# Expert routing beside matmuls: four-byte operands of full height for the search's products, and another order around the first routing

## The chip, the cores and the metric

The kernel runs on one core of a Trainium2 chip. The metric is the device time of one execution in microseconds (us). The engines have short names in the profile: PE is TensorE (matmuls; PEld is its weight loading), DVE is VectorE, ACT is ScalarE, POOL is GpSimd, and SP is SyncE, which issues most DMA transfers.

## What is computed

Three blocks follow each other over 3072 tokens of width 512. The first is a linear attention with decay. The second, which the change is about, gives each token to one of 8 experts, with at most 384 tokens for each expert, and runs that expert's two matmuls on them. The third is a rational activation between two more matmuls.

```python
def _moe_ref(x, w_gate, w1, w2):
    N, D = x.shape                       # 3072, 512
    E = w_gate.shape[1]; cap = N // E    # 8, 384
    flat = (x @ w_gate).flatten()
    order = np.argsort(-flat)
    assigned = -np.ones(N); counts = np.zeros(E)
    for idx in order:                    # best pairs of token and expert first
        tok, e = idx // E, idx % E
        if assigned[tok] >= 0 or counts[e] >= cap:
            continue
        assigned[tok] = e
        counts[e] += 1
    ...
    for e in range(E):
        h = np.maximum(x[assigned == e] @ w1[e], 0.0)
        out[assigned == e] = h @ w2[e]

# behind it, for all tokens: h = x @ w_in; P = a0 + a1 h + a2 h^2 + a3 h^3
# Q = 1 + |b0| |h| + |b1| h^2; result = (P / Q) @ w_out
```

## The kernel before

**The three stretches.** Up to about 180 us the attention runs, 24 blocks of 128 tokens. From about 180 to 202 us the first expert's tokens are found, with little else to do. From there on the eight experts follow each other, n = 0 to 7: each time 384 tokens are gathered from DRAM (`fetch`, one indirect DMA on POOL per 128 tokens), transposed on PE (`xt`), multiplied by `w1` (`mm1`, 8 pieces f of 12 matmuls) and `w2` (`mm2`, 8 pieces of 12), then by `w_in` (`mm3`, 16 pieces of 12), and, after the activation on ACT, DVE and POOL, by `w_out` (`mm4`, 16 pieces of 9). Each float32 operand is split in two parts of the type `float32r` (in the code `F32R`, four bytes a number, a rounded float32), so every product is made of three.

**The search.** An expert is full when 384 tokens have it as their best. `route(n)` finds the n-th expert that fills, and the score at which it does, bit by bit, because the greedy order is one threshold per expert. For n from 1 on, it takes 8 rounds of 4 bits, so 56 rounds in all; the searches follow each other without a pause, ahead of the experts that need them, and the last ends within expert 6. In a round DVE compares the scores of all tokens with 16 thresholds (`cm`, 128 x 24 x 16). PE counts per expert: three products with the one-hot `oh` as the weights, 64 columns wide (8 blocks times 8 experts, L609). DVE takes the diagonal (`cmk`), adds (`ce`) and spreads it (`ex`, 64 rows). PE sums over the 64 rows with a product whose weights are ones (`oneb[0:64]`, 128 columns, L623). DVE takes the largest, and sets the next threshold (`thr`, `pre`). After the 8 rounds come a pair of products for ranks (L660, L661), three for positions (L691) and one to spread the list (L707); the result is `idx`, the list of tokens, and `ei`, the expert's number.

**What sets the order.** PE, ACT and POOL execute in the order in which the code is written; DVE's order is chosen by a scheduler, and `tc.issue_after(x)` puts what it holds behind x. The search is a generator, `Chain`; a `hop` issues two of its steps, so that a round is two hops. `slot()` makes a hop after a piece of an expert's matmuls whenever a credit reaches 1. Before the slots begin, `HOPS0` says how many hops stand before the transposes of the first expert, after them, and after its first `mm1`.

**Other work beside the first expert.** Weights of `w_out` come as float64: `job_conv` turns a block into float32 (L240, L242, L243 on DVE, L241 on ACT), and `job_split` splits it (L246 on ACT, L247 on POOL). `w1_split` and `w2_split` do the same split for the expert's weights.

## Time and profile before

| | |
|---|---|
| median of 3 runs | 1106.55 us (1105.77 to 1111.75) |
| the profiled execution | 1109.52 us, of which the span of its instructions is 1107.6 us |
| PE | 1034.6 us busy (93%), 6278 matmuls |
| DVE, ACT, POOL | 792.7 us (72%), 697.4 us (63%), 635.3 us (57%) |
| the chain that ended last | PE 72%, of it the search's L609 and L623 1% each by the page |
| granted PE clock, mean | 0.971 |

The chain that ended last is followed back from the last instruction to what released each step; the shares are of the span. The granted clock is given as a share of 2.4 GHz: 1.00 is 2.4 and 0.50 is 1.2 GHz.

### The profile page before, as it was taken

Reading aid. Unit: us, or ns where it says so; the run is one execution under the profiler, and the core shown is the slowest. Engines: PE = TensorE matmul, PEld = TensorE weight load, DVE = VectorE, ACT = ScalarE, POOL = GpSimd, SP = SyncE. Lnnn points to the kernel's source line nnn. Section 1 sums busy time; section 2 is a strip of 40 time slices with the busy share of each in tenths; the row PEclk is TensorE's granted clock in tenths of the full one; section 3 lists DMA queues with packets and bytes.
Section 4 is the critical chain, followed back from the end, with each engine's and each line's share of the span. In section 5 each row is a group of like instructions: output and inputs, shape, how many; then the busy total and the mean of one; then the engine's idle time right before and its main releaser. Section 6 shows DMA issues by size and latency. Waiting matters only on the chain.

```text
span 1107.6 us, 18242 instructions
## 1 busy us (share of the span) xinstructions
PE 1034.6 (93%) x6278; PEld 918.2 (83%) x6278; DVE 792.7 (72%) x1850; ACT 697.4 (63%) x1365; POOL 635.3 (57%) x612
## 2 busy tenths in 40 slices
PE   6988985589999999999999999999999999999995
PEld 6877874478778988898889888988898889989994
DVE  5899897677985688568847874787578855761673
ACT  7988782245685387448844874478348735873783
POOL 5766762373586356635763566356636664666452
PEclk9999997599899999999999999999999999999998
DMA  9998862332334312331233123212321232224110
GB/s 195 239 259 219 215 163 87 115 124 77 97 109 129 105 39 86 103 98 39 86 105 95 39 86 112 89 44 81 115 86 58 67 115 86 59 67 124 57 58 28
DMA packets 142027, 115.00 MB, mean 104 GB/s; under 512 B 56560, under 2 KB 122352, under 8 KB 141936
## 3 DMA queue, kind: packets, MB, share of 16 engines
q1 hardware_dynamic: 131184, 76.10, 26.4%
q0 software_dynamic: 10752, 37.75, 10.5%
q8 instruction: 49, 0.80, 0.3%
q14 instruction: 42, 0.34, 0.1%
HBM read 98.10 MB, written 15.73 MB: 103 GB/s over the span
## 4 chain that ended last, share of the span: by engine, by line
PE 72%; DVE 5%; issue 1%; POOL 1%; DMA 1%; ACT 1%; POOLq 0%; DVEq 0%
PE w L795 35%; PE acc L888 22%; PE acc L795 12%; PE pr L609 1%; PE w L779 1%; PE pr L623 1%; DMA xg<-xd,idx 1%; DVE t L868 0%; DVE acc L867 0%; DVE t L851 0%; DVE t L850 0%; DVE qq L866 0%; POOL woh L247 0%; POOL qq L849 0%; DVE cm L573 0%
## 5 line engine op out<-in xcount | busy, mean ns | idle before, releaser
L888 PE MATMUL acc<-woh,hg 128*128 128x512 f32 x1152 | 292.7, 400 | 5.0 <-ACT hg L873 4.2
L888 PEld LDWEIGHTS acc<-woh,hg 128*128 128x128 f32 x1152 | 214.0, 189 | 49.6 <-ACT hg L873 5.4
L849 POOL TENSOR_TENSOR qq<-qq,z 128x384 f32<-128x384 f32 x127 | 128.9, 1015 | 164.7 <-ACT z L847 164.7
L874 POOL TENSOR_TENSOR hg<-t,hg 128x384 fp32r<-128x384 f32 x127 | 131.1, 1032 | 91.8 <-ACT hg L873 62.1
L795 PE MATMUL w<-yT,wih 128*128 128x384 f32 x960 | 178.6, 338 | 0.0
L795 PEld LDWEIGHTS w<-yT,wih 128*128 128x128 f32 x960 | 166.8, 188 | 4.6 <-DVE yT L820 0.2
L795 PE MATMUL w<-xT,w1s 128*128 128x384 f32 x768 | 152.4, 347 | 0.5 <-ACT xT L781 0.5
L795 PE MATMUL acc<-hg,w2s 128*128 128x384 f32 x768 | 148.5, 342 | 0.1
L795 PEld LDWEIGHTS w<-xT,w1s 128*128 128x128 f32 x768 | 135.8, 192 | 4.4 <-ACT xT L781 0.7
L795 PEld LDWEIGHTS acc<-hg,w2s 128*128 128x128 f32 x768 | 133.4, 189 | 3.4 <-DVE hg L804 0.5
L247 POOL TENSOR_TENSOR w1s<-w1r,w1s 128x512 fp32r<-128x512 f32 x64 | 83.3, 1301 | 71.9 <-ACT w1s L246 71.4
L247 POOL TENSOR_TENSOR w2s<-w2r,w2s 128x512 fp32r<-128x512 f32 x64 | 84.2, 1316 | 54.6 <-ACT w2s L246 54.4
L873 ACT ACTIVATE hg<-t 128x384 fp32r<-128x384 f32 x128 | 67.2, 525 | 75.6 <-DVE t L868 75.5
L866 DVE SCALAR_TENSOR_TENSOR qq<-qq,acc 128x384 f32<-128x384 f32 x128 | 70.8, 553 | 59.6 <-ACT acc L861 34.9
L795 PE MATMUL w<-yT,wis 128*128 128x384 f32 x576 | 111.1, 341 | 0.0
L795 PEld LDWEIGHTS w<-yT,wis 128*128 128x128 f32 x576 | 100.9, 189 | 2.8
L846 ACT ACTIVATE qq<-w,rb 128x384 f32<-128x384 f32 x128 | 73.1, 571 | 32.3 <-PE w L795 31.4
L803 ACT ACTIVATE hg<-w 128x384 fp32r<-128x384 f32 x64 | 31.3, 489 | 94.2 <-PE w L795 83.2
L850 DVE TENSOR_TENSOR t<-w,t 128x384 f32<-128x384 f32 x128 | 70.4, 550 | 23.8 <-ACT t L848 23.8
L246 ACT ACTIVATE w2s<-w2r 128x512 fp32r<-128x512 f32 x64 | 40.2, 629 | 73.9 <-POOL w1s L247 33.1
L848 ACT ACTIVATE t<-w,ab 128x384 f32<-128x384 f32 x128 | 86.1, 672 | 0.0
L860 ACT ACTIVATE z<-qq,qcb 128x384 f32<-128x384 f32 x128 | 77.5, 606 | 6.8 <-POOL qq L849 6.8
(174 smaller groups left out, 1731.1 us busy)
## 6 DMA issues: line engine op xcount, KB each, us to landing
wis<-wid POOLq DMA_DIRECT2D x42, 512.0 KB, 3.6
w1r<-in_moe_w_dram SPq DMA_DIRECT2D x64, 256.0 KB, 2.9
w2r<-in_moe_w_dram SPq DMA_DIRECT2D x64, 256.0 KB, 2.7
qn<-in_q_dram SPq DMA_DIRECT2D x48, 128.0 KB, 4.1
kn<-in_k_dram SPq DMA_DIRECT2D x24, 256.0 KB, 4.4
vn<-in_v_dram SPq DMA_DIRECT2D x24, 256.0 KB, 4.9
xd<-xn SPq DMA_DIRECT2D x48, 128.0 KB, 3.9
raw<-in_moe_w_in_dram SPq DMA_DIRECT2D x10, 512.0 KB, 5.6
```

Source lines behind the costliest of these rows:

```text
L246: nc.scalar.activation(dst[:, 0], src, AF.Copy)
L247: lo_eng.tensor_tensor(dst[:, 1], src, dst[:, 0].bitcast(F32), op=OP.subtract)
L795: nc.tensor.matmul(o, w[a], x[b], start=first and n[key] == 1, stop=last and n[key] == total)
L846: nc.scalar.activation(qq, p, AF.Square, scale=rb)
L848: nc.scalar.activation(t, p, AF.Identity, bias=ab[:, 2:3], scale=ab[:, 3:4])
L849: light(n, i).tensor_tensor(qq, qq, z, op=OP.add)
L850: nc.vector.tensor_tensor(t, p, t, op=OP.mult)
L860: nc.scalar.activation(z, qq, AF.Ln, bias=qcb)
L866: nc.vector.scalar_tensor_tensor(qq, qq, QC, r, op0=OP.add, op1=OP.mult)
L873: nc.scalar.activation(g[:, 0], t, AF.Copy)
L874: light(n, i).tensor_tensor(g[:, 1], t, g[:, 0].bitcast(F32), op=OP.subtract)
L888: nc.tensor.matmul(ACC[t], g[:, x, t * 128:(t + 1) * 128], woh[:, i, y], start=i == 0 and x + y == 0, stop=i == NF2 - 1 and x == 1)
```

## The change

For n from 1 on, the operands of the search's counting and summing products and of the rank products become `F32R`: new tiles `ohr` (one-hot), `oner` (ones), `umor` (a matrix for ranks), and `cm`, `ex` and `X` in the new type. `ex` gets 128 rows, of which the lower 64 are set to zero once, and the ones of the sum (`oner`) all 128 rows. The counting product keeps its 64 columns of weights. `pre` and, in the last round, the comparison with the capacity live in PSUM. For the first routing (n = 0) the two-byte types stay, and its thresholds move from PSUM to SBUF.

The order around the first routing is another: the updates of `Tm` and `Sl`, which prepare the next search, and the first step of the next search stand behind `idx`; the gathers stand ahead of the first splits; `HOPS0` goes from (3, 1, 1) to (1, 2, 1), one hop fewer in all; and each `job_conv(f)` stands behind the low part of the activation of piece f + 1 (`HLO`).

```diff
-HOPS0 = (3, 1, 1)
+HOPS0 = (1, 2, 1)
...
+    ppre = prb[:, 264:296].bitcast(I32)
...
+    oner = rt.tile([128, 128], F32R, name="oner")
+    umor = rt.tile([128, 128], F32R, name="umor")
+    ohr = rt.tile([128, NCH, E], F32R, name="ohr")
+    ex = rt.tile([128, E, 2 ** BITS_REST[0]], F32R, name="ex")
+    nc.vector.tensor_copy(ex[64:128].rearrange("p e j -> p (e j)"), zero[64:128, 0:1].to_broadcast([64, E * 2 ** BITS_REST[0]]))
+    nc.vector.tensor_copy(oner, oneb)
+    nc.vector.tensor_copy(umor, half("umo", BF16))
...
-            nc.vector.tensor_tensor(oh, t8, mraw[:, :, None].to_broadcast([128, NCH, E]), op=OP.is_equal)
+            nc.vector.tensor_tensor(ohr, t8, mraw[:, :, None].to_broadcast([128, NCH, E]), op=OP.is_equal)
...
-                    pre = rt.tile([128, J], I32, name="pre")
+                    pre = ppre[:, 0:J] if n else rt.tile([128, J], I32, name="pre")
...
-                thr = pthr[:, 32 * (i % 2):32 * (i % 2) + J]
+                thr = pthr[:, 32 * (i % 2):32 * (i % 2) + J] if n else rt.tile([128, J], I32, name="thr", bufs=2)
...
-                cm = rt.tile([128, NCH, J], BF16, name="cm")
+                cm = rt.tile([128, NCH, J], F32R if n else BF16, name="cm")
...
                 for g in range(3):
                     nc.tensor.matmul(pc.rearrange("p c j -> p (c j)"),
-                                     oh[:, 8 * g:8 * g + 8, :].rearrange("p c e -> p (c e)"),
+                                     ohr[:, 8 * g:8 * g + 8, :].rearrange("p c e -> p (c e)"),
                                      cm[:, 8 * g:8 * g + 8, :].rearrange("p c j -> p (c j)"),
...
-                ex = rt.tile([64, E, J], FP16, name="ex")
...
-                nc.vector.tensor_tensor(ex, ce[:, None, :].to_broadcast([64, E, J]),
+                nc.vector.tensor_tensor(ex[0:64], ce[:, None, :].to_broadcast([64, E, J]),
...
                 pd = pr(128, E, J)
-                nc.tensor.matmul(pd.rearrange("p e j -> p (e j)"), oneb[0:64, :], ex.rearrange("p e j -> p (e j)"),
+                nc.tensor.matmul(pd.rearrange("p e j -> p (e j)"), oner, ex.rearrange("p e j -> p (e j)"),
                                  start=True, stop=True)
...
-                    fe = rt.tile([128, E, J], F32, name="fe")
-                    nc.vector.tensor_scalar(fe, pd, float(CAP), None, op0=OP.is_ge)
+                    nc.vector.tensor_scalar(pd, pd, float(CAP), None, op0=OP.is_ge)
                     S = rt.tile([128, E], F32, name="S")
-                    nc.vector.tensor_reduce(S, fe, axis=AX.X, op=OP.add)
+                    nc.vector.tensor_reduce(S, pd, axis=AX.X, op=OP.add)
...
-        X = rt.tile([128, 2, NCH], BF16, name="X")
+        X = rt.tile([128, 2, NCH], F32R, name="X")
...
-        nc.tensor.matmul(pw[:, 0], half("umo", BF16), Xf, start=True, stop=True)
-        nc.tensor.matmul(pw[:, 1], oneb, Xf, start=True, stop=True)
+        nc.tensor.matmul(pw[:, 0], umor, Xf, start=True, stop=True)
+        nc.tensor.matmul(pw[:, 1], oner, Xf, start=True, stop=True)
...
-        eo = rt.tile([128, E], F32, name="eo")
-        nc.vector.tensor_scalar(eo, c8, em, None, op0=OP.is_equal)
-        nc.vector.tensor_scalar(sl[:, 0], u, float(CAP), BIG, op0=OP.is_lt, op1=OP.mult)
-        nc.vector.tensor_tensor(Tm, sl[:, 0], Tm, op=OP.add)
-        nc.vector.scalar_tensor_tensor(Sl, eo[:, None, :].to_broadcast([128, NCH, E]), BIG, Sl,
-                                       op0=OP.mult, op1=OP.add)
...
-        nc.vector.tensor_scalar(idx, ix, float(NT // 2), None, op0=OP.add)
+        LASTI[0] = nc.vector.tensor_scalar(idx, ix, float(NT // 2), None, op0=OP.add).ins
+
+        with tc.issue_after(LASTI[0]):
+            eo = rt.tile([128, E], F32, name="eo")
+            nc.vector.tensor_scalar(eo, c8, em, None, op0=OP.is_equal)
+            nc.vector.tensor_scalar(sl[:, 0], u, float(CAP), BIG, op0=OP.is_lt, op1=OP.mult)
+            nc.vector.tensor_tensor(Tm, sl[:, 0], Tm, op=OP.add)
+            nc.vector.scalar_tensor_tensor(Sl, eo[:, None, :].to_broadcast([128, NCH, E]), BIG, Sl,
+                                           op0=OP.mult, op1=OP.add)
...
-        nc.vector.scalar_tensor_tensor(h[:, 1], p, 0.0, h[:, 0].bitcast(F32), op0=OP.max, op1=OP.subtract)
+        HLO[n, f] = nc.vector.scalar_tensor_tensor(h[:, 1], p, 0.0, h[:, 0].bitcast(F32), op0=OP.max,
+                                                   op1=OP.subtract).ins
...
         pass
     begin(0)
+    for t in range(TB):
+        fetch(0, t)
     w1_split(0, 0)
     w1_split(0, 1)
-    for t in range(TB):
-        fetch(0, t)
     for f in range(2):
         w2_split(0, f)
-    chain = Chain()
+    with tc.issue_after(LASTI[0]):
+        chain = Chain()
...
             if n == 0:
                 job_split(f - 1)
-                job_conv(f)
+                with tc.issue_after(HLO[0, min(f + 1, NF1 - 1)]):
+                    job_conv(f)
```

On PE, around the first expert's transposes (`w<-cft,xg`): this is what stood there from the transposes on to the second `mm1` piece (`w<-xT,w1s`); L609 is the counting product, L623 the summing one.

```order
L779 MATMUL w<-cft,xg 128x128 x12
L623 LDWEIGHTS oneb
L623 MATMUL pr<-ex,oneb 128x128
L795 MATMUL w<-xT,w1s 128x384 x12
L609 LDWEIGHTS oh
L609 MATMUL pr<-cm,oh 64x128
L609 LDWEIGHTS oh
L609 MATMUL pr<-cm,oh 64x128
L609 LDWEIGHTS oh
L609 MATMUL pr<-cm,oh 64x128
L795 MATMUL w<-xT,w1s 128x384 x12
```

The same place on PE after the change, where L621 is the counting product, L634 the summing one, L791 the transposes and L807 the experts' products:

```order
L621 MATMUL pr<-cm,ohr 64x128 x3
L791 MATMUL w<-cft,xg 128x128 x12
L634 MATMUL pr<-ex,oner 128x128
L621 MATMUL pr<-cm,ohr 64x128 x3
L807 MATMUL w<-xT,w1s 128x384 x12
L634 MATMUL pr<-ex,oner 128x128
L807 MATMUL w<-xT,w1s 128x384 x12
```

A sum and a count now stand between the transposes and the first `mm1` piece, where only a sum stood; the separate weight loads are gone from the list, since a product of this type issues its own.

On POOL, between the last conversions of the attention stretch (`wih`) and the second expert weights (`w2s`), the gathers (`xg<-xd,idx`) move:

```order
 L247 TENSOR_TENSOR wih<-cv_2361,wih 128x512
 L247 TENSOR_TENSOR wih<-cv_2416,wih 128x512
+L756 DMA xg<-xd,idx 128x512 x3
 L247 TENSOR_TENSOR w1s<-w1r,w1s 128x512 x2
-L744 DMA xg<-xd,idx 128x512 x3
 L247 TENSOR_TENSOR w2s<-w2r,w2s 128x512 x2
```

They stood behind the two splits of `w1s`, and stand ahead of them.

On DVE, in the middle of the first expert (before): L804 is the low part of an `mm1` piece, L240, L242 and L243 are a `w_out` conversion, and the rest are the search's steps.

```order
L618 TENSOR_REDUCE ce<-cmk 64x16
L242 SCALAR_TENSOR_TENSOR xg<-yT,xg 128x512
L619 TENSOR_TENSOR ex<-ce,pr 64x128
L243 ISA xg<-xg 128x1024
L633 TENSOR_REDUCE fs<-pr 128x16
L240 TENSOR_SCALAR xg<-yT 128x512
L634 TENSOR_SCALAR fs,nf<-fs 128x15
L804 SCALAR_TENSOR_TENSOR hg<-w,hg 128x384
L567 SCALAR_TENSOR_TENSOR pr<-nf,pre 128x16
L242 SCALAR_TENSOR_TENSOR xg<-yT,xg 128x512
L573 TENSOR_TENSOR cm<-m,pr 128x384
```

The same conversion (the fifth) on DVE after the change, where L818 is the low part of the activation:

```order
L818 SCALAR_TENSOR_TENSOR hg<-w,hg 128x384
L628 TENSOR_TENSOR cmk<-pr,cft 64x128
L240 TENSOR_SCALAR xg<-yT 128x512
L629 TENSOR_REDUCE ce<-cmk 64x16
L242 SCALAR_TENSOR_TENSOR xg<-yT,xg 128x512
L630 TENSOR_TENSOR ex<-ce,pr 64x128
L643 TENSOR_REDUCE fs<-pr 128x16
L644 TENSOR_SCALAR fs,nf<-fs 128x15
L579 SCALAR_TENSOR_TENSOR pr<-nf,pr 128x16
L585 TENSOR_TENSOR cm<-m,pr 128x384
```

The conversion stood inside the threshold part of a round, and stands inside its counting part.

## Rows read from the trace of the kernel before

**Rows 1.** Windows: length, then PE, PEld, DVE, ACT, POOL busy (count), clock, DMA.

```profile
817.80:926.30 108.50, 108.50 (x577) 96.45 (x577) 74.31 (x188) 67.87 (x131) 62.36 (x63) 1.00 0.27 81
926.30:1027.80 101.50, 101.50 (x542) 94.91 (x541) 54.02 (x96) 67.74 (x131) 62.40 (x63) 1.00 0.26 79
```

**Rows 2.** Timeline of PE in expert 3: start us, duration us, what, count.

```profile
575.71 0.35 PE L609 MATMUL pr<-cm,oh 128*64 128x128 bf16 x3
...
580.75 0.35 PE L609 MATMUL pr<-cm,oh 128*64 128x128 bf16 x3
...
588.37 0.23 PE L623 MATMUL pr<-ex,oneb 64*128 64x128 f16 x1
...
590.74 2.25 PE L795 MATMUL acc<-hg,w2s 128*128 128x384 f32 x12
592.82 0.20 PE L660 MATMUL pr<-X,cit 128*128 128x48 bf16 x1
...
595.08 2.25 PE L795 MATMUL acc<-hg,w2s 128*128 128x384 f32 x12
```

**Rows 3.** Timeline of PE in expert 5, with four transposes.

```profile
877.18 2.26 PE L888 MATMUL acc<-woh,hg 128*128 128x512 f32 x9
879.28 0.60 PE L779 MATMUL w<-cft,xg 128*128 128x128 f32 x4
...
881.81 2.25 PE L888 MATMUL acc<-woh,hg 128*128 128x512 f32 x9
883.99 0.23 PE L623 MATMUL pr<-ex,oneb 64*128 64x128 f16 x1
```

**Rows 4.** Timeline of PE in the attention, two blocks, one without the L393 products.

```profile
63.03 1.68 PE L380 MATMUL pa<-QB,kh 128*128 128x256 f32 x12
64.64 0.69 PE L393 MATMUL ps<-vt,kn 128*64 128x64 f32 x16
65.26 1.19 PE L422 MATMUL pt<-IW,xt 128*128 128x136 f32 x8
66.29 1.05 PE L405 MATMUL py<-qt,Sb 128*128 128x128 f32 x8
...
85.14 1.66 PE L380 MATMUL pa<-QB,kh 128*128 128x256 f32 x12
86.64 1.09 PE L422 MATMUL pt<-IW,xt 128*128 128x136 f32 x8
87.57 1.05 PE L405 MATMUL py<-qt,Sb 128*128 128x128 f32 x8
```

**Rows 5.** Groups by form, whole span: count | busy us, mean ns | idle before.

```profile
L380 PE MATMUL pa<-QB,kh 128*128 128x256 f32 x288 | 43.6, 301 | 1.2 <-POOL QB L365 0.8 <-DVE kh L369 0.2
...
L422 PE MATMUL pt<-IW,xt 128*128 128x136 f32 x192 | 28.8, 294 | 0.7 <-ACT xt L412 0.7
```

**Rows 6.** Timeline, the first expert's start; in brackets idle time and its releaser.

```profile
201.64 0.19 DVE L714 TENSOR_SCALAR idx<-ix 128x3 int32<-128x3 f32 x1
...
203.31 0.29 DVE L633 TENSOR_REDUCE fs<-pr 128x16 f32<-128x128 f32 x1 [0.35 <-PE pr L623]
...
204.38 1.15 POOL L744 DMA_INDIRECT xg<-xd,idx  x1 [0.17 <-DVE pre L564]
204.49 0.55 DVE L573 TENSOR_TENSOR cm<-m,pr 128x384 bf16<-128x384 f32 x1
...
207.09 0.95 POOL L744 DMA_INDIRECT xg<-xd,idx  x1 [0.30 <-issue]
...
212.62 4.21 PE L795 MATMUL w<-xT,w1s 128*128 128x384 f32 x12 [0.47 <-ACT xT L781]
```

**Rows 7.** Windows beside the first expert: columns as in the first group.

```profile
241.20:245.30 4.10, 0.15 (x1) 0.11 (x1) 3.78 (x8) 1.71 (x3) 4.10 (x4) 0.93 0.11 42
245.30:252.74 7.44, 7.44 (x28) 7.02 (x27) 3.12 (x7) 0.49 (x1) 0.52 (x1) 0.58 0.00 0
```

**Rows 8.** Timeline of DVE in the first of these windows.

```profile
241.47 1.48 DVE L240 TENSOR_SCALAR xg<-yT 128x512 int32<-128x512 int32 x1 [0.99 <-POOL woh L247]
```

More of the change, by code (lines that the diff above doesn't have):

```diff
@@ L535, in pr @@
         return v
+    oner = rt.tile([128, 128], F32R, name="oner")
[5 more added lines that the diff above has]
+    nc.vector.tensor_copy(umor, half("umo", BF16))
     ROUTE = {}
+    LASTI = {}
     def route(n):
@@ L577, in route @@
                 o2, b2, _ = CI_OFF[tb, i + 1]
-                pre = rt.tile([128, 2 ** b2], I32, name="pre")
+                pre = ppre[:, 0:2 ** b2] if n else rt.tile([128, 2 ** b2], I32, name="pre")
                 nc.vector.tensor_tensor(pre, cit[:, o2:o2 + 2 ** b2], thr[:, 0:1].to_broadcast([128, 2 ** b2]),
@@ L693, in route @@
         yield
-        Zm = rt.tile([128, NB, 8], F32, name="Zm")
+        Zm = rt.tile([128, NB, 8], F32, name="cmk")
         Z = rt.tile([128, NB], FP16, name="Z")
@@ L795, in three @@
             nc.tensor.matmul(o, w[a], x[b], start=first and n[key] == 1, stop=last and n[key] == total)
+    HLO = {}
     def mm1(n, f):
```

## The prediction

> **What bounds the kernel now.** The first view to read is the windows that hold one expert's worth of work each, from one `yT` to the next. In the one from 817.80 PE is busy for all of its 108.50 us, while DVE has 74, ACT 68 and POOL 62 of them; the next one, which is the first without a search in it, takes 101.50 [rows 1]. So from about 300 us on PE sets the time, and a search costs it 7 us for each expert. What an edit is worth there is what it takes from PE's own sequence, and the timeline of PE shows that. The second view is the same timeline in the first expert, where PE does wait. One place matters: between 241.20 and 245.30 PE is busy for 0.15 us, and the next window has a granted clock of 0.58 (1.00 is 2.4 GHz, 0.50 is 1.2) [rows 7].
>
> **The price of a round now.** Two pieces of 12 expert products and one round of the search fill the time from one L609 to the next, 575.71 to 580.75, or 5.04 us [rows 2]. A piece with no search in it takes 2.08 (590.74 to 592.82) [rows 2]. The round therefore costs 5.04 - 2 x 2.08 = 0.88 us of PE. The products themselves last a fraction of that; most is how PE enters and leaves them. The part of L623: from its start to the next piece but one is 2.37 (588.37 to 590.74), that is 0.29 over a piece [rows 2], and the piece ahead of it is 0.08 longer than a plain one (2.18 from 881.81 to 883.99, against 2.10) [rows 3]. So L623 costs 0.37 and L609 0.51.
>
> **What makes them dear.** Both use part of the array: L609 has weights of 64 columns, L623 of 64 rows. Is it the part or the two-byte type? The attention has four-byte products with 64 columns of weights. Twelve L380 take 1.61 when such products follow (63.03 to 64.64), and 1.50 when full ones do (85.14 to 86.64); eight L422 take 1.03 behind them and 0.93 behind full ones (65.26 to 66.29, 86.64 to 87.57) [rows 4]. So with four bytes the step into 64 columns and out of it costs 0.11 + 0.10, as with two. This decides what the change can bring: it makes L623 a full 128 x 128 product, and leaves L609 at 64 columns.
>
> The Trainium skill (TensorEngine Tiling, Key Properties) has a rule that speaks against half of the change: a change of the tiling mode drains the array, and 128 x 64 is a mode of its own whatever the type. By that rule only the sum gains, 14 us in all as below; if the drain hung on the two-byte type, the count would gain too, and the sum would be 30 us. The four-byte rows agree with the rule.
>
> **The change part by part.**
>
> *The sum (now L634).* A full four-byte product of 128 columns is in the trace: four transposes L779 and two pieces take 4.63 (877.18 to 881.81), less 2.10 and 2.08 that is 0.45, so 0.11 each, with no entrance ahead of them [rows 3]. The sum falls from 0.37 to 0.11.
>
> *The count (now L621).* It keeps its 0.51, plus a little for four-byte weights of 64 columns: between 0 and 0.05, and I take 0.03, the middle. Together a round costs 0.65 in place of 0.88. The chain runs 7 searches of 8 rounds: 56 x 0.23 = 12.9 us.
>
> *The rank products.* The pair L660 and L661 costs 2.26 - 2.08 = 0.18 (592.82 to 595.08) [rows 2]; as two full four-byte products 0.22. Seven times that adds 0.3. The pair of routing 0 has PE idle around it.
>
> *DVE's side.* `cm`, `ohr` and `ex` are as many elements as before, from float32 sources; in the steady stretch DVE has 34 us free in 108.50 [rows 1], which also hides `pre` in PSUM and the comparison in place. Without that cover they would cost what they differ by, for which no row exists; I take nothing.
>
> *The start.* Three casts for the new tiles stand on DVE ahead of routing 0, in its path. The nearest rows are small DVE operations of 0.19 to 0.29 [rows 6]; times three, minus what overlaps, I take +0.4 (0 to 0.9). Behind it, the updates and the next search's first steps no longer stand between the products that make `idx`; they are eight to ten such operations, and some of them filled waits: -1.0 (0 to -2). The first gather, issued at 204.38 although `idx` ended at 201.83, no longer waits for two splits; at 1.36 apart (204.38 to 207.09) the third is issued near 203.9 in place of 207.09 [rows 6], and its data would allow the first expert product 3.2 earlier, near 209.4 in place of 212.62 [rows 6]. But PE's program now has a sum and a count between the transposes and that product. Behind the sum, DVE must make the next threshold and `cm`: 203.31 to 205.04, 1.73 us when nothing stands between [rows 6], and now low parts of `xT` do. From transposes that end near 208.9, sum, threshold and count end at 211.4 at the earliest. So what is late next is the search itself. I take 0.5 of the 3.2 as gained (0 to 3.2), the casts and the earlier `idx` included.
>
> *The conversions.* The wait at 241.20 costs 3.95, and then 24 expert products and one count run at a low clock: 7.44 against some 4.6, so 2.8 more; 6.8 in all [rows 7]. In it DVE holds L240, which waits for POOL's split until 241.47 and then takes 1.48 [rows 8], with the next threshold queued behind it, for which PE waits. Now each conversion stands behind the low part of a later piece, so POOL has more time ahead of it; but the fifth still stands in the middle of a round, between `cmk` and `ce`, and still needs POOL's split. Gone entirely: -6.8. The same wait at the sum instead of the count: 0 (a second one: +6.8). I take -1.0, nearer to no gain, since the order shows the wait moved and not removed. One hop fewer ahead shifts the search by one piece; it ends long before the next gathers, and I take 0.
>
> **Sum.** -12.9 + 0.3 - 0.5 - 1.0 = -14.1 us. The profiled execution took 1109.52 (span 1107.6), so it would become 1095.4; that execution was 3.0 over the median of 1106.55. From the median: 1092.5 us.
>
> **The rivals.**
>
> *Four passes (slower).* If a `float32r` product with fewer than 256 columns ran like plain float32, its price would be that of L422, which has 192 records for 24 x 4 products [rows 5], at 0.93 / 8 = 0.116 a record [rows 4]: 0.23 for 136 columns, 0.22 for 128. The three counts then rise by 0.16 each (from 0.055, a pass), the sum costs 0.22: 0.51 + 0.03 + 0.49 + 0.22 = 1.25 a round, 0.37 more than now, 20.7 us, and 1126 us. Against it: L380 with 256 columns of this type has one record a product (288 for 24 x 12) [rows 5] at 1.50 / 12 = 0.125 [rows 4], one pass. For it: no row has this type under 256 columns. It decides from between two and three passes on. The Trainium skill (FP8 and Floating Point Precision, TensorE Precision Notes) gives four passes to true FP32 and lists a reduced reading of four bytes apart from it; only the first would lead to this rival.
>
> *Two passes.* The counts rise by 0.05 each, the sum stays at 0.11 (which the weights' load may set anyway): 0.80 a round, -4.5, in all -5.7, 1101 us.
>
> *The first expert pays it back.* A second wait like that of 241 us, with its low clock: +6.8 and no 1.0 gained, 1100; two of them, 1107.
>
> *The count loses its drain too.* Then 0.51 would be near 0.25, 15 us more gained: 1078. The four-byte rows of 64 columns speak against it [rows 4].
>
> *The sum keeps its price,* because the step in and out hangs on something else than the shape: 1107. The transposes speak against it [rows 3].
>
> **Chances.** Forecast 0.66, four passes 0.12, two passes 0.08, the first expert pays back 0.06, sum unchanged 0.04, count without its drain 0.04. The forecast's own range is 1085 to 1100, from the bounds of the start and the conversions. The range 1083 to 1107 takes in the two passes and the paid-back case as well, and leaves out the four passes and the low end. A measurement of this kernel can tell about 0.5%, 5.5 us: faster than 1101 is the forecast, the count without its drain, half of two passes and half of the paid-back case, 0.77; slower is four passes, 0.12; the rest, 0.11, is the same.
>
> **What would show it.** Right: the step from one L621 to the next over two pieces falls from 5.04 to about 4.81; the piece ahead of L634 is plain and the window without a search stays at 101.5, the others fall by about 1.8. Wrong: three L621 that last 0.5 longer (passes), a piece behind L634 that is still 0.29 longer (the shape is not it), or a low granted clock at another place between 205 and 300 us.

## The result, and the profile after

The changed kernel takes 1088.70 us (median of 4 runs, 1087.29 to 1090.37), the kernel before on the same chip 1106.16; the ratio is 0.983, with a 95% interval of 0.981 to 0.985. The forecast was 1092.5. The size was nearly right, but for the wrong reasons in part: gains and losses that the forecast left out nearly cancel.

The profiled execution took 1087.82 us (span 1085.4). PE is busy for 1011.9 us in place of 1034.6. Windows of both kernels, first of before: from the first product of the first routing to the first product on `yT` of expert 0, from there to that of expert 1, and to that of expert 6 (columns as in [rows 1]).

```profile
180.45:260.14 79.69, 53.54 (x364) 47.45 (x365) 53.20 (x163) 22.74 (x42) 35.15 (x25) 0.73 0.34 106
260.14:381.16 121.02, 114.81 (x586) 98.51 (x585) 94.69 (x242) 73.40 (x143) 73.11 (x71) 0.97 0.35 107
381.16:927.11 545.95, 545.80 (x2895) 483.00 (x2895) 388.49 (x991) 338.41 (x651) 312.25 (x315) 1.00 0.28 84
```

And of after, with the windows of the last search and of the first expert without one, as [rows 1], and one behind the place of [rows 7]:

```profile
180.87:252.91 72.04, 50.14 (x363) 45.71 (x364) 53.08 (x158) 22.71 (x42) 34.11 (x25) 0.76 0.38 118
252.91:368.05 115.14, 109.56 (x587) 99.04 (x586) 91.17 (x235) 73.49 (x143) 74.59 (x71) 0.99 0.36 112
368.05:904.57 536.52, 531.01 (x2897) 488.31 (x2896) 386.45 (x1003) 337.71 (x651) 312.97 (x315) 1.00 0.28 86
...
798.90:904.57 105.67, 105.47 (x576) 97.44 (x575) 75.23 (x188) 67.62 (x131) 62.51 (x63) 1.00 0.28 83
904.57:1006.28 101.71, 101.71 (x542) 95.00 (x541) 54.02 (x96) 67.78 (x131) 62.35 (x63) 1.00 0.26 80
...
236.00:252.91 16.91, 14.57 (x87) 13.56 (x86) 14.62 (x36) 7.51 (x15) 10.78 (x8) 1.00 0.11 34
```

The first output comes 7.7 us sooner, the next expert takes 5.9 less, the five experts behind it (40 rounds) 9.4 less; the rest takes 180.5 and 180.8. An expert without a search takes 101.7, where [rows 1] had 101.5; the last one with a search takes 105.7, in place of 108.2 between the same two products (818.91 to 927.11). The low clock of [rows 7] is gone: 1.00 from 236 us on, with waits of PE of 1.31 and 0.97 there in place of one of 3.95. In the third window PE was busy for all but 0.15 us before, and is idle for 5.5 us after.

By the profiles the kernel is 21.7 us faster (1109.52 to 1087.82), by the medians 17.5: the profile of before lies 3.4 over its median, that of after 0.9 under. The stretch up to the first routing moves from one execution to the next (its last L422 starts between 174.6 and 179.5 us in the traces of this study), so parts are compared from the first routing on.

A count and a sum beside plain pieces of 2.08 (PE's timeline, after):

```profile
252.91 2.25 PE L807 MATMUL w<-yT,wih 128*128 128x384 f32 x12
255.00 0.22 PE L634 MATMUL pr<-ex,oner 128*128 128x128 f32 x1
255.06 4.38 PE L807 MATMUL w<-yT,wih 128*128 128x384 f32 x24
259.27 0.34 PE L621 MATMUL pr<-cm,ohr 128*64 128x128 f32 x3
259.45 2.30 PE L807 MATMUL w<-yT,wih 128*128 128x384 f32 x12
261.59 0.63 PE L903 MATMUL acc<-woh,hg 128*128 128x512 f32 x2
```

The piece ahead of L634 is plain (252.91 to 255.00), and the sum costs 259.27 - 255.00 - 2 x 2.08 = 0.11, as forecast. The count costs 261.59 - 259.27 - 2.08 = 0.24, where the forecast kept 0.54. The 40 rounds of the third window give about the same, from start to start less the plain pieces: sums 0.356 before and 0.123 after, counts 0.483 before and 0.227 after, the latter in the 29 rounds without a wait. So a round costs 0.35 in place of 0.84. That would be 40 x 0.49 = 19.6 us there; 9.4 came.

So where did 10 us go? In this window eleven counts come late. Eight of them stand in dense rounds, where one round of the search comes in every two pieces. PE's timeline, and DVE's for the same round:

```profile
446.47 0.22 PE L634 MATMUL pr<-ex,oner 128*128 128x128 f32 x1
...
448.90 0.40 PE L621 MATMUL pr<-cm,ohr 128*64 128x128 f32 x3
...
453.78 0.40 PE L621 MATMUL pr<-cm,ohr 128*64 128x128 f32 x3
```

```profile
446.73 0.29 DVE L643 TENSOR_REDUCE fs<-pr 128x16 f32<-128x128 f32 x1 [1.20 <-PE pr L634]
447.19 0.56 DVE L818 SCALAR_TENSOR_TENSOR hg<-w,hg 128x384 fp32r<-128x384 f32 x1 [0.17 <-ACT hg L817]
447.67 0.16 DVE L644 TENSOR_SCALAR_CACHE_REDUCE fs<-fs 128x15 f32<-128x15 f32 x1
...
448.08 0.55 DVE L585 TENSOR_TENSOR cm<-m,pr 128x384 fp32r<-128x384 f32 x1
448.67 0.18 DVE L591 TENSOR_TENSOR pr<-cit,pr 128x16 int32<-128x16 int32 x1
```

The step from count to count is 4.88 and not 2 x 2.08 + 0.35 = 4.5. DVE answers the sum late: the low part L818 stands between the maximum and the threshold, and the count begins 0.05 behind `pre` (L591), 0.27 behind the end of `cm`. In these rounds part of the saved PE time turned into a wait. It is not so in all of them: of the 13 dense steps in the window three take 4.88 or 4.89, three 4.75 and seven 4.55 to 4.68. The last include all those of experts 3 and 5, where L818 stands behind the count. Second, the waits of PE from 205 us on (us in total, how often, the longest; the short ones of the dense rounds are not in this view):

```profile
PE pr L621 <- DVE ohr L561: 4.7, 3, 2.1
PE pr L621 <- DVE pr L591: 4.3, 2, 3.0
```

Three first counts of a search wait 4.7 us for their one-hot. Two of them, with 2.6 us, stand in the third window, and one, with 2.1, in the second; the waits of the other line lie in the first. In the trace before no count waits behind 262 us. The updates of `Tm` and `Sl` stand behind `idx` in every search, not only in the first, and the one-hot behind them.

### The profile page after: what moved, and what is told of

Read it like the earlier page. It is cut to its first block, busy times and chain, and to the rows that moved or that the text cites. A ratio compares the mean times of both kernels' runs of the same rounds, so it can differ in the third digit from the quotient of the medians.

```text
span 1085.4 us, 18274 instructions
## 1 busy us (share of the span) xinstructions
PE 1011.9 (93%) x6278; PEld 923.2 (85%) x6278; DVE 787.6 (73%) x1853; ACT 696.7 (64%) x1365; POOL 636.2 (59%) x612
## 4 chain that ended last, share of the span: by engine, by line
PE 65%; DVE 6%; issue 1%; ACT 1%; POOL 0%; POOLq 0%; DVEq 0%
PE w L807 32%; PE acc L903 22%; PE acc L807 9%; PE pr L621 1%; PE w L791 1%; DVE cm L585 1%; DVE hg L818 1%; ACT hg L817 0%; DVE t L883 0%; DVE qq L881 0%; DVE t L865 0%; DVE acc L882 0%; PE pr L634 0%; DVE idx L718 0%; DVE X L665 0%
## 5 line engine op out<-in xcount | busy, mean ns | idle before, releaser
L903 PE MATMUL acc<-woh,hg 128*128 128x512 f32 x1152 | 292.0, 399 | 3.0 <-ACT hg L888 2.8
L903 PEld LDWEIGHTS acc<-woh,hg 128*128 128x128 f32 x1152 | 213.9, 189 | 47.2 <-ACT hg L888 4.5
L807 PE MATMUL w<-yT,wih 128*128 128x384 f32 x960 | 179.3, 339 | 1.1 <-DVE yT L835 0.9
L807 PEld LDWEIGHTS w<-yT,wih 128*128 128x128 f32 x960 | 166.6, 188 | 4.7 <-DVE yT L835 1.2
L807 PE MATMUL w<-xT,w1s 128*128 128x384 f32 x768 | 148.2, 341 | 0.0
L807 PE MATMUL acc<-hg,w2s 128*128 128x384 f32 x768 | 145.7, 338 | 0.0
L807 PEld LDWEIGHTS w<-xT,w1s 128*128 128x128 f32 x768 | 134.2, 190 | 1.0
L807 PEld LDWEIGHTS acc<-hg,w2s 128*128 128x128 f32 x768 | 132.3, 188 | 0.6
L807 PE MATMUL w<-yT,wis 128*128 128x384 f32 x576 | 109.7, 338 | 1.3 <-DVE t L866 1.3
L807 PEld LDWEIGHTS w<-yT,wis 128*128 128x128 f32 x576 | 100.8, 188 | 4.4 <-DVE t L866 1.5
```

What stands on the lines that cost most here:

```text
L807: nc.tensor.matmul(o, w[a], x[b], start=first and n[key] == 1, stop=last and n[key] == total)
L903: nc.tensor.matmul(ACC[t], g[:, x, t * 128:(t + 1) * 128], woh[:, i, y], start=i == 0 and x + y == 0, stop=i == NF2 - 1 and x == 1)
```

## The experiments

The table shows, for each, the median and the ratio to the kernel before on the same chip, and from its trace, in us: from the first routing to the list of tokens (end of `idx`), from the first routing to the first product on `yT` of expert 0 (the first output), and the two windows that follow, one expert and five experts long (as above). The kernel before was run again beside each group of kernels; the row `before` has the median of the first group.

| kernel | us | ratio, 95% | list | 1st output | next | five |
|---|---|---|---|---|---|---|
| before | 1106.16 | | 21.38 | 79.69 | 121.0 | 545.95 |
| after | 1088.70 | 0.983 (0.981-0.985) | 18.07 | 72.04 | 115.1 | 536.52 |
| count_two_byte | 1099.76 | 0.992 (0.990-0.995) | 18.03 | 70.78 | 116.8 | 546.25 |
| sum_half_height | 1104.44 | 0.996 (0.994-0.998) | 18.05 | 76.03 | 117.1 | 546.72 |
| sum_two_byte | 1087.96 | 0.981 (0.977-0.985) | 18.04 | 72.22 | 115.4 | 536.41 |
| order_only | 1106.42 | 0.999 (0.997-1.000) | 17.65 | 70.97 | 118.0 | 553.26 |
| types_only | 1090.28 | 0.983 (0.978-0.987) | 18.99 | 77.95 | 116.1 | 529.89 |
| thr_psum | 1089.66 | 0.984 (0.980-0.988) | 20.63 | 73.94 | 114.9 | 536.43 |
| conv_old | 1091.90 | 0.986 (0.984-0.988) | 18.04 | 77.76 | 114.9 | 536.43 |
| thr_sbuf | 1105.53 | 0.999 (0.996-1.001) | 18.04 | 75.20 | 120.3 | 548.63 |
| pre_later | 1090.35 | 0.985 (0.983-0.987) | 18.03 | 75.06 | 114.7 | 536.15 |
| updates_free | 1085.33 | 0.980 (0.977-0.983) | 18.05 | 71.36 | 115.2 | 531.89 |
| free_later | 1084.56 | 0.980 (0.978-0.982) | 18.03 | 75.77 | 114.5 | 531.66 |
| low_late | 1082.85 | 0.977 (0.974-0.979) | 18.02 | 72.39 | 116.1 | 529.76 |

**The count in two bytes.**

```diff
-            nc.vector.tensor_tensor(ohr, t8, mraw[:, :, None].to_broadcast([128, NCH, E]), op=OP.is_equal)
+            nc.vector.tensor_tensor(oh, t8, mraw[:, :, None].to_broadcast([128, NCH, E]), op=OP.is_equal)
...
-                cm = rt.tile([128, NCH, J], F32R if n else BF16, name="cm")
+                cm = rt.tile([128, NCH, J], BF16, name="cm")
...
-                                     ohr[:, 8 * g:8 * g + 8, :].rearrange("p c e -> p (c e)"),
+                                     oh[:, 8 * g:8 * g + 8, :].rearrange("p c e -> p (c e)"),
```

> The changed kernel, with the counting products in two bytes again (one-hot and comparisons in bf16, 64 columns of weights); the sum, the ranks and the order stay. The prediction's step: the price of a count hangs on its 64 columns, so 0.51 us before and after; then this kernel takes what the changed one takes, 1088 to 1089 us. But in the trace after, the product ahead of a count is 0.177 us long in place of 0.268, and a count costs about 0.26. Theory A (the price belongs to two-byte products on a part of the array): the step ahead of the first count is 0.268 again, a count without a wait costs 0.49, and the kernel takes 8 to 12 us more, 1097 to 1101 us; less than 56 x 0.25 = 14, since in the dense rounds a wait for VectorE of about 0.3 us lies at the same place. Theory B (what fell is not the type but something in the order of the instructions): no change, 1089 us, and 0.177 ahead of a count.

**The sum over 64 rows in four bytes.**

```diff
-                nc.tensor.matmul(pd.rearrange("p e j -> p (e j)"), oner, ex.rearrange("p e j -> p (e j)"),
+                nc.tensor.matmul(pd.rearrange("p e j -> p (e j)"), oner[0:64, :], ex[0:64].rearrange("p e j -> p (e j)"),
```

> The changed kernel, with the summing product over 64 rows again, in four bytes. If the price of the sum hangs on the 64 rows (the prediction's step): 0.27 us ahead of it and 0.36 us a round in place of 0.11, so 10 to 14 us more, 1099 to 1103 us. Theory A (two bytes and a part of the array are both needed): 0.11 a round as with the full height, 1088 to 1089 us.

**The sum over 128 rows in two bytes.**

```diff
-    ex = rt.tile([128, E, 2 ** BITS_REST[0]], F32R, name="ex")
+    ex = rt.tile([128, E, 2 ** BITS_REST[0]], FP16, name="ex")
...
-                nc.tensor.matmul(pd.rearrange("p e j -> p (e j)"), oner, ex.rearrange("p e j -> p (e j)"),
+                nc.tensor.matmul(pd.rearrange("p e j -> p (e j)"), oneb, ex.rearrange("p e j -> p (e j)"),
```

> The changed kernel, with the summing product in fp16 and bf16 again, but over all 128 rows, the lower 64 of them zero. The prediction's step (the shape) and theory A (two bytes on a part) both say: no price ahead of it, some 0.13 us a round as the two-byte product that spreads the list has now, so 1 us more, 1089 to 1091 us. Theory C (any two-byte product between four-byte ones pays to enter): 0.36 a round, 10 to 14 us more, 1099 to 1103 us.

PE's timelines of the same kind of place in the three: a piece of mm4, the product in question, a piece of mm3, the next mm4 (4.19 without a product between). First count_two_byte (L620 is the count), whose sum is the changed kernel's (L633):

```profile
606.57 2.26 PE L902 MATMUL acc<-woh,hg 128*128 128x512 f32 x9
608.67 0.22 PE L633 MATMUL pr<-ex,oner 128*128 128x128 f32 x1
...
610.88 2.27 PE L902 MATMUL acc<-woh,hg 128*128 128x512 f32 x9
...
615.07 2.26 PE L902 MATMUL acc<-woh,hg 128*128 128x512 f32 x9
617.26 0.35 PE L620 MATMUL pr<-cm,oh 128*64 128x128 bf16 x3
...
619.74 2.27 PE L902 MATMUL acc<-woh,hg 128*128 128x512 f32 x9
```

sum_half_height, with its sum and a count in four bytes:

```profile
613.73 2.26 PE L903 MATMUL acc<-woh,hg 128*128 128x512 f32 x9
615.92 0.32 PE L634 MATMUL pr<-ex,oner 64*128 64x128 f32 x1
...
618.36 2.27 PE L903 MATMUL acc<-woh,hg 128*128 128x512 f32 x9
...
622.56 2.26 PE L903 MATMUL acc<-woh,hg 128*128 128x512 f32 x9
624.65 0.34 PE L621 MATMUL pr<-cm,ohr 128*64 128x128 f32 x3
...
626.98 2.27 PE L903 MATMUL acc<-woh,hg 128*128 128x512 f32 x9
```

sum_two_byte:

```profile
620.01 2.26 PE L903 MATMUL acc<-woh,hg 128*128 128x512 f32 x9
622.11 0.23 PE L634 MATMUL pr<-ex,oneb 128*128 128x128 f16 x1
...
624.32 2.27 PE L903 MATMUL acc<-woh,hg 128*128 128x512 f32 x9
```

From piece to piece, less 4.19: the count costs 619.74 - 615.07 - 4.19 = 0.48 in two bytes and 626.98 - 622.56 - 4.19 = 0.23 in four. The sum costs 0.44 over 64 rows in four bytes (618.36 - 613.73), and 0.12 over 128 rows in four bytes (610.88 - 606.57) and in two (624.32 - 620.01). So for the sum it is the height alone, as the prediction had it, and theory A falls there; for the count it is the type, at the same 64 columns, and there the prediction's step and theory B fall. The two times follow: 11 and 16 us more than the changed kernel's, or 10 and 14 by the ratios to the kernel before, as was expected, while the sum in two bytes at full height is the same within its interval.

**The order alone, and the types alone.** The first is the kernel before with the new order and the new places of thresholds and `pre`; the second is the changed kernel with the old order (updates ahead of the last products of the list, old `HOPS0`, gathers behind the splits, `job_conv` unordered). Both keep one small edit that the diff of the change leaves out: `Zm`, in the making of the list, takes the buffer of `cmk`. Of the first, and then of the second, against the changed kernel:

```diff
-                cm = rt.tile([128, NCH, J], F32R if n else BF16, name="cm")
+                cm = rt.tile([128, NCH, J], BF16, name="cm")
...
+                ex = rt.tile([64, E, J], FP16, name="ex")
...
-        X = rt.tile([128, 2, NCH], F32R, name="X")
+        X = rt.tile([128, 2, NCH], BF16, name="X")
...
```

```diff
-HOPS0 = (1, 2, 1)
+HOPS0 = (3, 1, 1)
...
-        with tc.issue_after(LASTI[0]):
-            eo = rt.tile([128, E], F32, name="eo")
...
-    with tc.issue_after(LASTI[0]):
-        chain = Chain()
+    chain = Chain()
...
```

> The kernel before with all of the new order and the new places of thresholds, and with the old types and heights. The prediction gave the order 1.5 us of 14. In the traces the first expert's output is ready 7.2 us earlier after the change, of which six or seven rounds in new types are some 3; against that, the first count of three later searches waits 4.7 us in sum for its one-hot, since the updates stand behind the list of tokens. Theory D (order gains at the start and loses in the steady stretch): about -4 + 4 = 0, 1103 to 1107 us, with waits for the one-hot in the trace. Rival (the order is a plain gain and the types give the rest): 1099 to 1102 us, without such waits.

> The kernel before with the new types, heights and places of thresholds, and the old order around the first routing (updates ahead of the list's last products, gathers behind the splits, three hops first, conversions where they stood). Theory D: without the updates behind the list, the waits for the one-hot in the steady stretch (2.1, 0.8 and 1.8 us) are gone, while the first expert loses some 4; together 1086 to 1090 us, about the changed kernel. Rival (the order is a plain gain of 4 or more): 1093 to 1096 us.

Theory D holds: order_only has its first output 8.7 us sooner than before and needs 7.3 more in the five windows, with the same 4.7 us of first counts that wait for the one-hot; it takes 1106.42, which is not told apart from the kernel before. types_only has no such waits and the best five windows of the two (529.9), but its first output is 5.9 later than the changed kernel's; 1090.28. Beside the first expert, where PE waits anyway, the cheaper rounds gave nothing: order_only has its first output at 70.97, and the changed kernel at 72.04. Of the 16.1 us which the types and heights are worth in the five windows, the order takes 6.6 back.

**The first routing's thresholds in PSUM again.**

```diff
-                thr = pthr[:, 32 * (i % 2):32 * (i % 2) + J] if n else rt.tile([128, J], I32, name="thr", bufs=2)
+                thr = pthr[:, 32 * (i % 2):32 * (i % 2) + J]
```

> The changed kernel, with the thresholds of the first routing in PSUM again, in the bank into which the counts are written. In the trace before, TensorE's counts of the first routing wait until all three comparisons and the next table have read the thresholds (1.5 us a round); after, they begin behind the first comparison (0.74 us). Theory E (the wait is for the bank): the waits of 1.5 us are back, the list of tokens is 2.4 to 3.5 us later, and the kernel takes 1.5 to 3.5 us more, 1090 to 1092 us. Rival (the list is earlier because the updates stand behind it): no change, 1089 us.

PE's timeline of the first routing, after and then thr_psum:

```profile
183.50 0.16 PE L612 MATMUL pr<-fl,oneq 32*128 32x1 bf16 x1 [0.26 <-DVE fe L607]
184.40 1.05 PE L599 MATMUL pr<-oh,cm 128*32 128x8 bf16 x24 [0.74 <-DVE cm L585]
```

```profile
185.24 0.16 PE L612 MATMUL pr<-fl,oneq 32*128 32x1 bf16 x1 [0.26 <-DVE fe L607]
186.91 0.78 PE L599 MATMUL pr<-oh,cm 128*32 128x8 bf16 x24 [1.51 <-DVE pre L591]
```

The wait of 1.51 is back, and its releaser is `pre`, which reads the thresholds, and not the comparison that the product needs. The list comes 2.56 us later and the first output 1.90. The whole, from the first routing on, is 906.1 in place of 904.5 us; the medians (1089.66 and 1088.70) don't tell that apart.

**The conversions where they stood.**

```diff
-                with tc.issue_after(HLO[0, min(f + 1, NF1 - 1)]):
-                    job_conv(f)
+                job_conv(f)
```

> The changed kernel without the order of the conversions: each job_conv where VectorE's scheduler puts it, as before. The prediction gave this order 1.0 us of a possible 6.8. By the prediction: 1 us more, 1089 to 1090 us. Theory F (this order removed the wait of 3.95 us and the low clock behind it): the output of the first expert is 4 to 7 us later, 1092 to 1096 us, with a wait of over 3 us ahead of a count near 240 us and a granted clock near 0.6 behind it.

PE's timeline of conv_old, and the window behind the wait:

```profile
246.18 0.47 PE L634 MATMUL pr<-ex,oner 128*128 128x128 f32 x1 [3.25 <-DVE ex L630]
246.45 4.15 PE L807 MATMUL w<-xT,w1s 128*128 128x384 f32 x12
250.40 3.17 PE L807 MATMUL acc<-hg,w2s 128*128 128x384 f32 x12
```

```profile
246.18:253.40 7.22, 7.22 (x25) 7.18 (x26) 3.47 (x10) 0.49 (x1) 0.48 (x1) 0.57 0.00 0
```

The wait is there (at the sum now), the clock of 0.57 behind it (near 1.2 GHz) too, and the first output comes 5.7 us later. By the trace theory F holds, and the 1.0 of the prediction was far too low. The median rose by 3.2 us only, and the intervals of the two ratios meet, so the times alone don't show it.

**Thresholds and `pre` in SBUF for the later searches.**

```diff
-                    pre = ppre[:, 0:J] if n else rt.tile([128, J], I32, name="pre")
+                    pre = rt.tile([128, J], I32, name="pre")
...
-                thr = pthr[:, 32 * (i % 2):32 * (i % 2) + J] if n else rt.tile([128, J], I32, name="thr", bufs=2)
+                thr = rt.tile([128, J], I32, name="thr", bufs=2)
...
-                pre = ppre[:, 0:2 ** b2] if n else rt.tile([128, 2 ** b2], I32, name="pre")
+                pre = rt.tile([128, 2 ** b2], I32, name="pre")
```

> The changed kernel, with the thresholds and the tables of the later searches in SBUF as well. In the dense rounds of the trace after, a count begins 0.05 us after the next table (pre) is written, which is 0.21 us after the comparison that it needs; both lie in the bank that the count writes to. Theory E: the counts there begin 0.2 us earlier, some 13 rounds, 2 to 3 us less, 1086 to 1087 us. Rival (the wait only moves to the sum that follows): no change, 1088 to 1089 us.

Neither was right: it takes 17 us more than the changed kernel. DVE's and POOL's timelines of a dense round of thr_sbuf:

```profile
360.25 1.13 DVE L579 SCALAR_TENSOR_TENSOR thr<-nf,pre 128x16 int32<-128x16 int32 x1
```

```profile
360.07 1.28 POOL L247 TENSOR_TENSOR w1s<-w1r,w1s 128x512 fp32r<-128x512 f32 x1 [1.12 <-ACT w1s L246]
```

The threshold's 16 columns take 1.13 us and end 0.03 behind POOL's split (361.38 and 361.35). By line, this instruction (least, median, longest in ns) in thr_sbuf, then in the changed kernel, then in the kernel before, where `pre` was in SBUF and only the threshold in PSUM:

```profile
L579 DVE SCALAR_TENSOR_TENSOR thr<-nf,pre x49: 160/354/1784, 212.4 to 905.7; 128x16 int32<-128x16 int32 x49
```

```profile
L579 DVE SCALAR_TENSOR_TENSOR pr<-nf,pr x49: 165/178/180, 209.8 to 883.5; 128x16 int32<-128x16 int32 x49
```

```profile
L567 DVE SCALAR_TENSOR_TENSOR pr<-nf,pre x49: 166/183/2414, 204.3 to 903.2; 128x16 int32<-128x16 int32 x49
```

With one of its inputs in PSUM it never lasts over 0.18. With both in SBUF it lasts over 0.25 us in 27 of 49 cases in thr_sbuf and in 12 of 49 before, and each of these 39 ends at most 0.05 behind an instruction of POOL. In thr_sbuf 14 of the comparisons (`cm`) are longer too, up to 2.19 us in place of 0.55. The Trainium skill (SBUF — State Buffer, section "SBUF: two separate sides") says that a VectorE instruction with two SBUF inputs and one of GpSimd that reads SBUF exclude each other for their whole length; the traces agree (1.13 us in place of 0.18, and the end 0.03 behind POOL's). The gain that theory E looked for is in the same trace, the count 0.05 behind `cm` and not behind `pre`, but is far smaller than the loss.

**`pre` behind the count, in PSUM.**

```diff
-            if 0 < i < len(bits) - 1:
+            if n == 0 and 0 < i < len(bits) - 1:
...
                                      start=g == 0, stop=g == 2)
                 yield
+                if 0 < i < len(bits) - 1:
+                    o2, b2, _ = CI_OFF[tb, i + 1]
+                    pre = ppre[:, 0:2 ** b2] if n else rt.tile([128, 2 ** b2], I32, name="pre")
+                    nc.vector.tensor_tensor(pre, cit[:, o2:o2 + 2 ** b2], thr[:, 0:1].to_broadcast([128, 2 ** b2]),
+                                            op=OP.bitwise_xor)
```

> The changed kernel, with the table for the next thresholds (pre) of the later searches computed behind the counting products, just ahead of cmk, and not ahead of them; it stays in PSUM, since with thresholds and tables in SBUF the threshold's own instruction took 1.13 us in place of 0.18 in the dense rounds. Theory E (a count waits for whatever VectorE still does in the bank that it writes to): a count that waits begins 0.05 us after the comparison and not after the table, 0.21 us earlier; in some 13 rounds, 2 to 3 us less, 1085.5 to 1087 us. Rival (the table's 0.18 us then stands ahead of cmk, and the sum waits instead): no change, 1088 to 1089 us.

The rival holds: the five windows are the same (536.2 against 536.5), and the time is 1090.35. No count of a dense round waits, but sums of dense rounds wait in their place (steps of up to 4.86), and the first output comes 3.0 us later. Shortening one side of a loop that passes through both engines moved the wait.

**The updates behind the list for the first routing only.**

```diff
-        with tc.issue_after(LASTI[0]):
+        with nullcontext() if n else tc.issue_after(LASTI[0]):
             eo = rt.tile([128, E], F32, name="eo")
```

> The changed kernel, with the updates of the scores put behind the list of tokens for the first routing alone; for the seven later ones VectorE's scheduler is free again. Theory D: the waits of the first counts for the one-hot (2.1, 0.8 and 1.8 us in the trace after) are gone, 3 to 5 us less, 1084 to 1086 us. Rival (the one-hot is late anyway, since the activation's work stands between): no change, 1089 us.

> The changed kernel with both edits: the updates behind the list for the first routing alone, and the table for the next thresholds behind the count. If the two waits are apart: the 4.7 us of the one-hot and 2 to 3 us of the dense rounds, 1081 to 1083 us. Rival (with the first count earlier the rounds fall elsewhere, and a wait comes back): as with the first edit alone, 1085 us.

In updates_free the first count of no later search waits for its one-hot any more, and the five windows fall by 4.6 us; theory D holds, 1085.33. In free_later `pre` behind the count adds nothing to it in the five windows (531.7 and 531.9) and has the first output 4.4 us later, as its own run had shown; the rival holds, 1084.56.

**The low part behind the comparisons.** updates_free, and for the later experts `mm1` leaves its low part (L818) to `mm1_low`; `LASTC[0]` is the last `cm` that was issued:

```diff
-                mm1(n, f + 2)
+                mm1(n, f + 2, n == 0)
                 slot(0)
+                if n:
+                    with tc.issue_after(LASTC[0]):
+                        mm1_low(n, f + 2)
```

> The changed kernel with the updates behind the list for the first routing alone, and in addition, for the later experts, the low part of an mm1 piece behind the comparisons of the search's step that follows the piece. In the dense rounds of the trace after, this low part stands on VectorE between the maximum of the sums and the next threshold, which then starts some 0.6 us later, and the count waits 0.2 to 0.3 us for it. Theory G (VectorE's order makes these waits): in the five windows from the second output of an expert to the seventh no count waits, the step between two counts of a dense round goes from 4.87 to about 4.5 us, and the five windows, 531.9 us with the first edit alone, fall to 527 to 529; 1081 to 1083 us in all. Rival (the loop of the search is too long for two pieces anyway, and the wait comes back at the sum): 1085 us, and a step of 4.8.

DVE's and PE's timelines of a dense round (L828 is the low part, L586 `cm`, L622 the count):

```profile
350.09 0.29 DVE L644 TENSOR_REDUCE fs<-pr 128x16 f32<-128x128 f32 x1 [2.39 <-PE pr L635]
350.41 0.17 DVE L645 TENSOR_SCALAR_CACHE_REDUCE fs<-fs 128x15 f32<-128x15 f32 x1
...
350.84 0.56 DVE L586 TENSOR_TENSOR cm<-m,pr 128x384 fp32r<-128x384 f32 x1
351.31 0.55 DVE L828 SCALAR_TENSOR_TENSOR hg<-w,hg 128x384 fp32r<-128x384 f32 x1
```

```profile
352.05 0.35 PE L622 MATMUL pr<-cm,ohr 128*64 128x128 f32 x3
...
356.59 0.35 PE L622 MATMUL pr<-cm,ohr 128*64 128x128 f32 x3
```

The step is 4.54, and in the five windows no count waits, with dense steps of 4.53 to 4.64. They take 529.8 us, 2.1 less than in updates_free and a little over what was expected. At 1082.85 us (0.977, 0.974 to 0.979) this version is faster than the changed kernel, but not shown to be faster than updates_free: the intervals of the ratios overlap, and from the first routing on its trace takes 899.0 us against 899.2, since the stretch to the first output and the window behind it take 1.9 more.

## Why the prediction was nearly right, and where not

**The sum** (0.37 to 0.11): right, and for its reason, the height. Its price was read from [rows 3], though, where the transposes take plain float32, and a transpose is another kind of product. That the `float32r` sum costs the same 0.11 was luck, as far as a row could tell.

**The count** ("keeps its 0.51"): this step failed. It measured 0.23 after 0.48, 56 x 0.25 = 14 us that the forecast left out, and the 0.03 that it added for four-byte weights is nowhere seen; the mechanism is that of the rival "the count loses its drain too". The step rested on [rows 4], four-byte products with 64 columns that pay. Those products (L393) differ from L621 in two ways. They take plain float32, with two records for each product (16 for 8), where `float32r` has one (3 for 3). And they write to the upper and the lower 64 partitions in turn, where L621 writes to the lower alone. I read them as the same case; which of the two explains their price wasn't tried. The lower half alone is not enough, since the count in two bytes writes there as well, and pays. The Trainium skill's rule (TensorEngine Tiling (Array Packing), Key Properties) that a change of the tiling mode drains the array fits the sum (0.44 over 64 rows, 0.12 over 128). The count in four bytes shows no such price: 0.23, with a plain piece ahead of it.

**DVE's side** ("I take nothing", since DVE has 34 us free): failed as well. Free time in a window says nothing of the loop sum, threshold, comparison, count. With PE faster by 0.5 a round, that loop ends last in some of the dense rounds (4.88 against 4.5). Low_late shows it: another place of one DVE instruction, and the wait is gone. And the new place of `pre` that I passed over has a price where it is missing: with thresholds and `pre` in SBUF the whole gain is lost. Which of the two makes the most of it wasn't separated by a run; in the trace of thr_sbuf the long thresholds last 22.5 us more than usual in all, and the long comparisons 15.0.

**The start** (-0.5): what it priced came out near. The casts (+0.4) show as 0.38, by which the first routing's first product starts later behind the last L422 (4.80 in place of 4.42). For `idx` it took -1.0, and -0.92 was measured (18.99 in types_only, 18.07). And what is late next is the search: the count ahead of the first `mm1` piece has the wait of 3.0 us for `pre` that the view of PE's waits shows. Without the conversions the order brings the first output 0.2 us sooner (77.95 in types_only, 77.76 in conv_old). Not in the sum at all were the thresholds of the first routing in SBUF, -2.56 at the list and -1.90 at the first output. The change named them; I gave them no price. Nor did I see that the updates stand behind `idx` in all searches, +4.6 us in the five windows.

**The conversions** (-1.0): mis-sized; 5.7 at the first output, nearly the bound of 6.8. The wait of 3.95 was removed, not moved.

**The rank products** (+0.3): a pair without a wait costs 0.26 in place of 0.18, 0.5 to 0.6 in all for seven; two of the five pairs in the third window wait besides.

**The sum of it.** From the first routing on the traces differ by 22.6 us (927.1 to 904.5), and the forecast's parts gave 14.1. It left out gains of 14.6 in the rounds (a round lost 0.49 and not 0.23, 56 times), 4.7 at the conversions and 1.9 by the thresholds, which makes 35.3. So some 12.7 us were given back, and that the total came near the forecast is luck. In the five windows 19.6 should have come and 9.4 did. Of the 10.2 between them the late counts hold some 5, the rank products 1.2, and idles ahead of L807 and L903 some 2; the rest is spread too thin to be named. Updates_free has 4.6 of them back, and low_late 6.8. The remaining 2.5 lie ahead of these windows, where PE waits beside the first expert and a cheaper round need not be time gained. Steps near the 4.81 that the prediction gave as its sign are found in the trace (4.75 to 4.89), but for the wrong reason: by a wait, and not by a price that the count kept.

Of the 22.6, the medians show 17.5 (21.2 for sum_two_byte, whose trace is the same within 0.4 us from the routing on). A median less the span from the routing on is 179.1 to 182.1 for the kernel before in five series, and 180.6 to 186.1 for the others. So something ahead of the routing seems to be slower by some 3 us, if the span behind it is the same in every execution, which one trace of each kernel can't show. The casts don't explain it: order_only has none, and gives 183.7. This is left open.

## What to carry to other kernels

When a product on the bound engine gets cheaper, look at the loop that it belongs to: here what another engine does between two of its steps was next, and the order on that engine, not its free time, decided. An order that is meant for one place (the first routing) belongs under that condition, for in the other seven searches it cost what it had won. And a row serves as evidence for a product only if it is alike in everything that could matter: the exact type (PE's rows write f32 for float32 and for `float32r`, and here the records for each product told them apart), and the half of the output written.

## What the runs showed of the hardware

- Beside full `float32r` products, one over 64 rows pays in two bytes (0.36) and in `float32r` (0.44); one over 128 rows pays in neither (0.12). Three products with 64 columns of weights cost 0.48 in two bytes and 0.23 in `float32r`, where the piece ahead of them stays plain.
- A VectorE instruction of 0.18 us lasts up to 1.78 us (thr_sbuf) and 2.41 (before) when both its inputs lie in SBUF, and each of the 39 long ones ends at most 0.05 behind an instruction of GpSimd; with one input in PSUM it never lasts over 0.18 (after).
- A count waits for the last VectorE access to the PSUM bank that it writes, in other columns too: 1.51 us in place of 0.74 in the first routing. The wait is one of the program; whether the chip needs it, no run shows.
